# The first batch's keys turned on TensorE, and routing in two places per batch of a retention and expert kernel

## The chip, the core and the metric

The kernel runs on one core of one Trainium2 chip. The metric is the device time of one execution in microseconds (us). The program is built once and timed in several runs, of which the median is given; one more execution is recorded by the hardware profiler. The engines are TensorE (PE; its weight loads are shown apart as PEld), VectorE (DVE), ScalarE (ACT), GpSimd (POOL) and SyncE (SP), which here only issues transfers.

## The reference

Two stages follow each other. The first is a retention: causal scores with a decay per head and no softmax. The second sends each token to one of eight experts. All is float32.

```python
def _attn_ref(q, k, v):                       # q, k, v: (8, 8, 576, 64)
    scores = scale * np.matmul(q, k.transpose(0, 1, 3, 2))
    gamma = 1.0 - 2.0 ** (-5.0 - np.arange(H, dtype=np.float32))
    Dmat = np.where(rel >= 0, gamma[:, None, None] ** rel[None, :, :], 0.0)
    return np.matmul(scores * Dmat[None], v)

def _moe_ref(x, expert_emb, tau, w1, w2):     # x: (4608, 512), 8 experts, F = 1024
    logits = normalised(x) @ normalised(expert_emb).T / tau
    expert_idx = np.argmax(logits, axis=1)
    gate_w = softmax(logits)[arange, expert_idx]
    for e in range(E):
        mask = expert_idx == e
        h = np.maximum(x[mask] @ w1[e], 0.0)
        out[mask] = gate_w[mask, None] * (h @ w2[e])
```

## The kernel before

**Data.** The host lays out `qk`, in which queries and keys stand transposed (the two heads of a pair by 64 features on the 128 partitions, 576 positions along), and `kv`, in which keys and values stand by position, in chunks of 128 positions. So the keys come twice: transposed, for the scores, and by position, in the tile `kt`, for the prefix sums of k times v.

**Retention.** It runs over 8 batches `b` and in each over 4 pairs of heads `p`. `emit_A(b, p)` makes the scores within chunks of 128 positions (L563, 16 matmuls) and masks them on VectorE (L572). `emit_U(b)` multiplies keys by position with values (L590, 64 matmuls) and sums over chunks on VectorE (L602, L604) to the states `Tst`. `emit_O(b, p)` multiplies masked scores by values (L620) and states by queries (L629), and VectorE scales and stores the result (L638, or L640 and L641). `emit_At` and `emit_Ot` are the same for the last 64 positions (L650, L652; L665, L668). `scale_v(b + 1)` on GpSimd multiplies the next batch's values by decays (L547, L551), as soon as they have landed. `emit_A` for the next pair stands ahead of `emit_O` for this one, and `emit_U(b + 1)` stands at the end of batch `b`.

**Routing.** The tokens of batch `b` are routed while batch `b + 1` runs, 4 tiles of 128 tokens for even `b` and 5 for odd `b`. `route_tasks(b)` lists the tasks. `route_logits` (L707, copy L710) and `route_turn` (L720, reduction L723) give the logits by token. `route_head` is six short VectorE operations (L174 to L182) that find the expert. `route_tile` turns one tile of tokens (L687), copies it on ScalarE (L691), stores it to memory through SP (L693) and sums its squares (L695). `route_rank` counts how many tokens stand ahead of each in its expert (matmuls L233 to L237, then L240 to L260 on VectorE). `route_onehot` makes the one-hot matrices `bt`, `ra` and `rp` on VectorE (L276, L268, L283), and `route_table` multiplies them (L296) and adds the product to the slot table `tab` (L305, L307). Ranks and table go on from batch to batch, so they must be made in order of the batches.

**Where the tasks stand.** After each pair of a batch before the last, three tasks are taken from the list: logits, head and tile 0 after pair 0; rank with one-hots and two tiles after pair 1; the rest and the table after pair 2. In the last batch `POPS` = 6, 3, 4, 0 tasks are taken ahead of `emit_O`: the list of batch 6 there ends with the slots of the first three groups of expert 0, three gathers of their tokens (L335) and `route_bump`. Behind the last batch the gathered tokens are turned (`xprep`, L365) and the experts' stage begins (L392 and L836).

**What sets the order.** The kernel is written in a tile framework. It takes the instructions in program order as their priority, and puts them on each engine's queue by a model of when each is ready; so an instruction can come ahead of one that is written before it. Each engine runs its queue in order. Tiles come from pools with fixed numbers of buffers; PSUM tiles named `m` (three buffers), `a` (three) and `o` (two) matter here. The expert weights' first four pieces (`wsplit_tasks(0)`, L145, L148, L149) stand in batches 1 and 2.

Of the kernel before, what the change touches and what calls it, by code (L numbers as in the profile page):

```python
# [9 lines left out]
F32 = mybir.dt.float32  # L10
# [8 lines left out]
P = 128  # L19
B, H, S, D = 8, 8, 576, 64  # L20
NP = H // 2
NCH = 4
# [19 lines left out]
EPOS = 2  # L42
OA = None
LAG = (3, 1)
POPS = (6, 3, 4, 0)
NO = NT + 2


# [32 lines left out]
def retention_moe(ctx: ExitStack, tc: tile.TileContext, qk, kv, embT, tau, w1, w2, cst, out):  # L81
    nc = tc.nc
# [8 lines left out]
    psm = ctx.enter_context(tc.tile_pool(name="psm", bufs=3, space=PSUM))  # L91
# [31 lines left out]
    ident = keep.tile([P, P], F32, name="ident")  # L123
# [139 lines left out]
    def route_onehot(b):  # L263

        t0, G = group_tiles(b)
        ai = grp[b][0]
        bt = sm.tile([P, 5, P], BF16, name="bt", bufs=1)[:, :G]
        nc.vector.tensor_tensor(  # L268
            out=bt,
            in0=ai[:, 1].unsqueeze(2).broadcast_to([P, G, P]),  # L270
            in1=cc("iota").unsqueeze(1).broadcast_to([P, G, P]),
            op=ALU.is_equal,
        )
        ra = sm.tile([P, 5, NE, CT], F32, name="ra", bufs=1)[:, :G]
        held = cc("iota")[:, : NE * (CT + 1)].rearrange("p (e i) -> p e i", e=NE)[:, :, :CT]
        nc.vector.tensor_tensor(  # L276
            out=ra,
            in0=ai[:, 0].unsqueeze(2).unsqueeze(3).broadcast_to([P, G, NE, CT]),
            in1=held.unsqueeze(1).broadcast_to([P, G, NE, CT]),
            op=ALU.is_equal,  # L280
        )
        rp = sm.tile([P, 5, 2, NA], BF16, name="rp", bufs=1)[:, :G]
        nc.vector.tensor_tensor(  # L283
            out=rp,
            in0=ra.rearrange("p g e i -> p g (e i)").unsqueeze(2).broadcast_to([P, G, 2, NA]),
            in1=entry[:, t0 : t0 + G].unsqueeze(3).broadcast_to([P, G, 2, NA]),
            op=ALU.mult,
        )
        grp[b] = (bt, rp)
# [137 lines left out]
    with ExitStack() as att:  # L427
# [12 lines left out]
        kt, vt_ = {}, {}  # L440
        KW = NCH * DM

        def load_k(b):
            t = a1.tile([P, KW], F32, name="kt", bufs=2)
            nc.sync.dma_start(out=t, in_=kv[b, :, :KW])
            kt[b] = t
# [16 lines left out]
        load_v(0, True)  # L463
        load_qk(0, 3)
        nc.sync.dma_start(out=cs[:, _FIRST:], in_=cst[:, _FIRST:])
        load_k(0)
        nc.sync.dma_start(out=emb, in_=embT)
        nc.sync.dma_start(out=taub, in_=tau.rearrange("(o n) -> o n", o=1).broadcast_to([P, 1]))

# [63 lines left out]
        def kview(b):  # L533
            return kt[b].rearrange("p (c n) -> p c n", c=NCH)
# [7 lines left out]
        def scale_v(b):  # L542
            eng = nc.vector if b == 0 else nc.gpsimd
            g = cc("gneg").rearrange("p (c h) -> p c h", c=NCH)
            v = vview(b)
            for c in range(NCH):
                eng.tensor_tensor(  # L547
                    out=v[:, c], in0=v[:, c], in1=g[:, c].unsqueeze(2).broadcast_to([P, H, D]), op=ALU.mult
                )
            vt = vtview(b)  # L550
            eng.tensor_tensor(  # L551
                out=vt, in0=vt, in1=cc("gnegt").unsqueeze(2).broadcast_to([P, NP, D]), op=ALU.mult
            )

        Pm, Pt = {}, {}

# [142 lines left out]
        def route_logits(b):  # L699

            x = xT[b, "x"]
            lt = a1.tile([P, 5 * P], F32, name="lt")
            parts = [(x, 0, 512)] if b % 2 == 0 else [(x, P, 512), (xC[b // 2], 0, P)]
            for src, o, n in parts:
                ps = psm.tile([P, 512], F32, name="m")
                for p in range(NP):
                    nc.tensor.matmul(  # L707
                        ps[p * EW : (p + 1) * EW, :n], E32[:, p, :], src[:, p, :], start=True, stop=True
                    )
                nc.scalar.copy(lt[:, o : o + n], ps[:, :n])  # L710
            ltb[b] = lt

        def route_turn(b):
            t0, G = group_tiles(b)
            lt = ltb.pop(b)
            for g0 in range(0, G, 4):
                gn = min(4, G - g0)
                ps = psm.tile([P, 512], F32, name="m")
                for g in range(gn):
                    nc.tensor.transpose(  # L720
                        ps[:, g * P : (g + 1) * P], lt[:, (g0 + g) * P : (g0 + g + 1) * P], ident
                    )
                nc.vector.tensor_reduce(  # L723
                    out=L_all[:, t0 + g0 : t0 + g0 + gn, :],
                    in_=ps[:, : gn * P].rearrange("p (g r e) -> p g e r", g=gn, r=NP)[:, :, :NE, :],
                    axis=AX.X,
                    op=ALU.add,
                )


        def route_tasks(b):
            G = group_tiles(b)[1]
            tiles = [lambda g=g: route_tile(b, g) for g in range(G)]
            logits = lambda: (route_logits(b), route_turn(b))
            head = lambda: route_head(b)
            rank, table = (lambda: (route_rank(b), route_onehot(b))), (lambda: route_table(b))
            if b == B - 2:
                t = [logits] + tiles[:2] + [head, rank] + tiles[2:] + [table, lambda: slots_to_tokens(0, 3)]
                t += [lambda i=i: gather(0, i, group_tiles(B - 1)[0] * P) for i in range(3)]
                return t + [route_bump]  # L740
            return [logits, head, tiles[0], rank] + tiles[1:] + [table]

        tasks = []
        wq = wsplit_tasks(0)
# [5 lines left out]
        for b in range(B):  # L750
            for p in range(NP):
                if b + 1 < B:
                    load_qk(b + 1, p)
                    if p == 0:
                        load_v(b + 1)
                        load_k(b + 1)
                        scale_v(b + 1)
                if p + 1 < NP:
                    if b > 0 or p == 2:
                        emit_A(b, p + 1)  # L760
                else:
                    if b + 1 < B:
                        emit_A(b + 1, 0)
                    emit_At(b)
                    if b + 1 < B:
                        emit_U(b + 1)
                if b == 0 and p == 0:
                    emit_U(0)
                if b == 0 and p == EPOS:
                    build_E()  # L770
                for _ in range(POPS[p] if b == B - 1 else 0):
                    if tasks:
                        tasks.pop(0)()
                emit_O(b, p)
                if p == NP - 1:
                    emit_Ot(b)
                for _ in range(3 if b < B - 1 else 0):
                    if tasks:
                        tasks.pop(0)()
                if b > 0 and p % 2 == 1 and wq:  # L780
                    wq.pop(0)()
            if b < B - 1:
                tasks += route_tasks(b)
# [306 lines left out]
```

## Time and profile before

| | us |
|---|---|
| median of 3 runs | 639.4 (639.04 to 642.41) |
| profiled execution | 639.75 |
| span in its profile | 637.8 |
| TensorE matmul busy | 618.2 (97%) |
| VectorE busy | 366.7 (57%) |
| ScalarE busy | 215.5 (34%) |
| GpSimd busy | 188.8 (30%) |

The retention stage takes up the span to about 176 us; the experts' stage fills the rest. Busy time of an engine is an average over both, so a stage has to be read by its own stretch. In the rows, a bracket behind an instruction tells how long its engine had been idle before it and what ended the wait; "x16" is a merged group of 16 instructions of which the first number is the start and the second the time from the first one's start to the last one's end. The granted clock is given as a share of TensorE's full speed, 2.4 GHz; 0.5 is 1.2 GHz.

### The profile page before, as it was taken

The numbers are of one execution on the slowest core, as the hardware profiler recorded it, in microseconds if no ns is written. First come the engines' busy times: TensorE is split into PE (matmuls) and PEld (weight loads), VectorE is DVE, ScalarE is ACT, GpSimd is POOL, SyncE is SP. The second block draws the span as 40 slices with busy tenths as digits, with TensorE's granted clock in tenths as the row PEclk, the third lists the DMA queues.
The fourth block names the chain that finished last, engine by engine and source line by source line (L and its number), as shares of the span: only waits on it lengthen the run. The fifth ranks groups of instructions, "written<-read, shape, count | busy, mean of one in ns | idle before, by whom it ended". The sixth has DMA issues, their size and how long they took to land. (4 is left out here: it accounts for less than half of the span.)

```text
span 637.8 us, 12644 instructions
## 1 busy us (share of the span) xinstructions
PE 618.2 (97%) x5257; PEld 551.8 (87%) x5257; DVE 366.7 (57%) x711; ACT 215.5 (34%) x393; POOL 188.8 (30%) x167
## 2 busy tenths in 40 slices
PE   8889899999999999999999999999999999999996
PEld 7768788788889889988988998898899889889985
DVE  5799988889758676660681466158146615812200
ACT  0032433223354536432442443244244324422211
POOL 3530322032126646313503322250332225020011
PEclk9999899999999999999999999999999999999999
DMA  8778889665356697492465148246514824500001
GB/s 321 302 251 334 309 324 330 253 249 205 120 160 198 188 240 250 118 264 94 110 151 218 57 116 268 84 116 172 208 33 117 281 82 116 149 37 23 1 34 43
DMA packets 73419, 110.46 MB, mean 173 GB/s; under 512 B 44650, under 2 KB 45070, under 8 KB 71440
## 3 DMA queue, kind: packets, MB, share of 16 engines
q1 hardware_dynamic: 65680, 89.68, 43.9%
q0 software_dynamic: 7680, 19.95, 9.6%
q8 instruction: 42, 0.69, 0.4%
q14 instruction: 17, 0.14, 0.1%
HBM read 81.01 MB, written 19.94 MB: 158 GB/s over the span
## 5 line engine op out<-in xcount | busy, mean ns | idle before, releaser
L392 PE MATMUL a<-xs,wslot 128*128 128x384 f32 (+1 forms) x1536 | 228.3, 310 | 0.4 <-DVE hs L810 0.4
L392 PEld LDWEIGHTS a<-xs,wslot 128*128 128x128 f32 x1536 | 225.9, 189 | 1.5 <-DVE hs L810 0.8
L836 PE MATMUL o<-wslot,hs 128*128 128x512 f32 (+1 forms) x984 | 222.0, 386 | 0.0
L836 PEld LDWEIGHTS o<-wslot,hs 128*128 128x128 f32 x984 | 181.1, 188 | 38.3
L810 DVE SCALAR_TENSOR_TENSOR hs<-a,hs 128x384 fp32r<-128x384 f32 (+1 forms) x128 | 62.8, 491 | 169.5 <-ACT hs L809 167.0
L844 POOL DMA_INDIRECT out<-y,sid x40 | 43.4, 1084 | 221.9 <-ACT y L843 188.2
L809 ACT ACTIVATE hs<-a 128x384 fp32r<-128x384 f32 (+1 forms) x128 | 56.1, 439 | 125.8 <-PE a L392 119.7
L149 DVE TENSOR_TENSOR wslot<-raw,wslot 128x1024 fp32r<-128x1024 f32 x64 | 78.3, 1223 | 27.7 <-ACT wslot L148 27.0
L148 ACT CAST wslot<-raw 128x1024 fp32r<-128x1024 f32 x64 | 66.8, 1044 | 53.1 <-DMA raw<-w 53.1
L335 POOL DMA_INDIRECT raw<-xd,gid x40 | 44.1, 1104 | 90.8 <-DVE wslot L149 42.0
L843 ACT ACTIVATE y<-o,gt 128x512 f32<-128x512 f32 (+1 forms) x41 | 27.7, 677 | 110.2 <-PE o L836 89.1
L547 POOL TENSOR_TENSOR vt<-vt,cs 128x512 f32<-128x512 f32 x28 | 29.8, 1092 | 90.5 <-DMA vt<-kv 36.5
L346 POOL DMA_INDIRECT gt<-gd,gid x40 | 50.0, 1251 | 12.2 <-issue 12.2
L563 PE MATMUL a<-qkt 64*128 64x128 f32 x512 | 43.1, 293 | 0.5 <-DMA qkt<-qk 0.3
L572 DVE TENSOR_TENSOR raw<-a,tri 128x512 f32<-128x512 f32 x64 | 41.0, 682 | 3.3 <-PE a L563 3.1
L563 PEld LDWEIGHTS a<-qkt 64*128 64x128 f32 x512 | 35.4, 192 | 7.9 <-issue 6.3
L620 PE MATMUL o<-raw,vt 128*64 128x128 f32 x512 | 36.1, 279 | 0.7 <-DVE raw L572 0.5
L620 PEld LDWEIGHTS o<-raw,vt 128*64 128x64 f32 x512 | 27.9, 136 | 5.0 <-issue 1.2
L710 ACT COPY lt<-m 128x512 f32<-128x512 f32 (+1 forms) x12 | 5.4, 481 | 78.5 <-PE m L707 78.5
L380 DVE COPY raw<-raw 128x1024 uint16<-128x1024 uint16 x37 | 28.3, 785 | 1.8 <-DMA raw<-raw 1.7
L691 ACT COPY y<-m 128x512 f32<-128x512 f32 x34 | 19.0, 587 | 29.9 <-PE m L687 28.3
L629 PE MATMUL o<-qkt,Tst 128*64 128x128 f32 x384 | 28.4, 274 | 0.0
(131 smaller groups left out, 442.8 us busy)
## 6 DMA issues: line engine op xcount, KB each, us to landing
raw<-w SPq DMA_DIRECT2D x64, 512.0 KB
qkt<-qk SPq DMA_DIRECT2D x32, 576.0 KB
xd<-y SPq DMA_DIRECT2D x36, 256.0 KB
kt<-kv SPq DMA_DIRECT2D x8, 1024.0 KB
vt<-kv SPq DMA_DIRECT2D x7, 1152.0 KB
vt<-kv SPq DMA_DIRECT2D x4, 256.0 KB
raw<-xd,gid POOLq DMA_INDIRECT x40
gt<-gd,gid POOLq DMA_INDIRECT x40
```

The source lines that it names most:

```text
L148: nc.scalar.copy(hi, raw)
L149: nc.vector.tensor_tensor(out=sl[:, 1, c * 1024 : (c + 1) * 1024], in0=raw, in1=hi.bitcast(F32), op=ALU.subtract)
L335: return nc.gpsimd.indirect_dma_start(out=t[:, :DM], out_offset=None, in_=xd[:rows, :], in_offset=bass.IndirectOffsetOnAxis(ap=gid[:, a : ...
L346: nc.gpsimd.indirect_dma_start(out=g[:, i : i + 1], out_offset=None, in_=gd[:, :], in_offset=bass.IndirectOffsetOnAxis(ap=gid[:, a : a + 1 ...
L392: nc.tensor.matmul(ps[:, :n], w[:, ws, d, f * P : (f + 1) * P], x[:, xsp, d, :], start=(d == 0 and k == 0), stop=(d == NP - 1 and k == 2),)
L563: nc.tensor.matmul(ps[h][:, c * P : (c + 1) * P], t[hs, 1, c * P : (c + 1) * P], t[hs, 0, c * P : (c + 1) * P], start=True, stop=True,)
L572: nc.vector.tensor_tensor(out=pm[:, h], in0=ps[h].rearrange("p (c n) -> p c n", c=NCH), in1=tri.unsqueeze(1).broadcast_to([P, NCH, P]), op ...
L620: nc.tensor.matmul(po[h * D : (h + 1) * D, c * P : (c + 1) * P], v[:, c, 2 * p + h, :], pm[:, h, c, :], start=(c == 0), stop=False,)
L809: a = nc.scalar.activation(hi, ps[:, :n], AF.Relu)
L810: v = nc.vector.scalar_tensor_tensor(out=hs[:, 1, f, o : o + n], in0=ps[:, :n], scalar=0.0, in1=hi.bitcast(F32), op0=ALU.max, op1=ALU.subt ...
L836: nc.tensor.matmul(ps[:, :step], hs[:, hsp, f, i * P : (i + 1) * P], w[:, ws, f, n : n + step], start=(f == 0 and k == 0), stop=(f == NF - ...
L844: nc.gpsimd.indirect_dma_start(out=out[:, :], out_offset=bass.IndirectOffsetOnAxis(ap=sid[:, a : a + 1], axis=0), in_=y, in_offset=None, b ...
```

## The change

`kt[0]`, the first batch's keys by position, is no longer loaded. The tile stays, and `turn_k` fills it: for each pair, four transposes on TensorE of the keys in `qkt[0, p]` into one PSUM tile and one copy on ScalarE. It stands at batch 0, pair 0, ahead of `emit_U(0)`.

The routing tasks of a batch now stand at two pairs of the next one, `SLOTS` = 0 and 2. At pair 0: rank and one-hots of the batch *before* the one that is being routed, then logits and tiles 0 and 1. At pair 2: the table of the batch before, then turn, head and the rest of the tiles. So rank, one-hots and table come a batch later than head and tiles. The list of batch 6, which runs in the last batch, takes batch 5's rank and table in as well, and `POPS` is 8 in place of 6.

```diff
-POPS = (6, 3, 4, 0)
+POPS = (8, 3, 4, 0)
+SLOTS = (0, 2)
...
-        load_k(0)
+        kt[0] = a1.tile([P, KW], F32, name="kt", bufs=2)
...
+        def turn_k(p):
+
+            ps = psm.tile([P, 512], F32, name="m")
+            for c in range(NCH):
+                nc.tensor.transpose(ps[:, c * P : (c + 1) * P], qkt[0, p][:, 1, c * P : (c + 1) * P], ident)
+            nc.scalar.copy(kview(0)[:, :, p * P : (p + 1) * P], ps.rearrange("p (c n) -> p c n", c=NCH))
...
+        owed = []
+
         def route_tasks(b):
             G = group_tiles(b)[1]
             tiles = [lambda g=g: route_tile(b, g) for g in range(G)]
-            logits = lambda: (route_logits(b), route_turn(b))
             head = lambda: route_head(b)
             rank, table = (lambda: (route_rank(b), route_onehot(b))), (lambda: route_table(b))
+            own = [lambda: route_logits(b)] + tiles[:2], [lambda: route_turn(b), head] + tiles[2:]
+
+            first, second = owed or ([], [])
+            owed[:] = [rank], [table]
             if b == B - 2:
-                t = [logits] + tiles[:2] + [head, rank] + tiles[2:] + [table, lambda: slots_to_tokens(0, 3)]
+                t = first + [lambda: (route_logits(b), route_turn(b))] + second + tiles[:2] + [head, rank]
+                t += tiles[2:] + [table, lambda: slots_to_tokens(0, 3)]
                 t += [lambda i=i: gather(0, i, group_tiles(B - 1)[0] * P) for i in range(3)]
                 return t + [route_bump]
-            return [logits, head, tiles[0], rank] + tiles[1:] + [table]
+            return [first + own[0], second + own[1]]
...
                 if b == 0 and p == 0:
+                    for r in range(NP):
+                        turn_k(r)
                     emit_U(0)
...
-                for _ in range(3 if b < B - 1 else 0):
-                    if tasks:
-                        tasks.pop(0)()
+                if b < B - 1 and p in SLOTS and tasks:
+                    for task in tasks.pop(0):
+                        task()
```

## Rows read from the trace of the kernel before

**Rows 1.** Page, part 1: busy us, share of the span, instructions, by engine.
```profile
PE 618.2 (97%) x5257; PEld 551.8 (87%) x5257; DVE 366.7 (57%) x711; ACT 215.5 (34%) x393; POOL 188.8 (30%) x167
```

**Rows 2.** Busy time by stretches, one per batch; last three: clock, DMA share, GB/s.
```profile
33.08:54.11 21.03, 19.74 (x324) 16.51 (x324) 19.95 (x46) 6.67 (x14) 5.15 (x5) 1.00 0.85 303
54.11:77.91 23.80, 22.07 (x342) 18.82 (x340) 22.57 (x49) 8.90 (x19) 5.36 (x5) 0.93 0.88 312
77.91:96.80 18.89, 18.80 (x327) 16.05 (x325) 16.47 (x45) 6.67 (x14) 4.68 (x5) 1.00 0.84 304
96.80:118.63 21.83, 20.32 (x342) 17.37 (x341) 18.89 (x43) 7.00 (x17) 5.67 (x5) 1.00 0.75 273
...
137.52:159.12 21.60, 20.32 (x343) 17.37 (x341) 18.66 (x43) 6.91 (x17) 4.75 (x5) 1.00 0.62 227
```

**Rows 3.** Groups by line, TensorE: busy us, mean ns, idle us before, releaser.
```profile
L296 PE MATMUL m<-rp,bt 128*128 128x80 bf16 x36 | 2.6, 203 | 5.6 <-DVE rp L283 5.6
```

**Rows 4.** Timeline, five tiles routed: start us, us, engine, line, operation.
```profile
107.53 4.77 POOL L547 TENSOR_TENSOR vt<-vt,cs 128x512 f32<-128x512 f32 x4 [13.11 <-PE m L687]
...
111.32 1.41 DVE L283 TENSOR_TENSOR rp<-ra,entry 128x400 bf16<-128x400 f32 x1
...
112.79 0.35 PE L296 MATMUL m<-rp,bt 128*128 128x80 bf16 x5 [1.49 <-DVE rp L283]
...
113.07 1.47 PE L563 MATMUL a<-qkt 64*128 64x128 f32 x16
```

**Rows 5.** Timeline, four tiles routed.
```profile
89.74 4.11 POOL L547 TENSOR_TENSOR vt<-vt,cs 128x512 f32<-128x512 f32 x4 [19.78 <-DMA vt<-kv]
...
90.82 0.42 PEld L687 LDWEIGHTS m<-ident,xT 128*128 128x128 f32 x4 [0.17 <-issue]
...
91.32 0.31 PE L296 MATMUL m<-rp,bt 128*128 128x80 bf16 x4
...
91.55 1.16 PE L563 MATMUL a<-qkt 64*128 64x128 f32 x16
```

**Rows 6.** Busy time behind one of the stops, columns as in rows 2.
```profile
70.45:74.90 4.45, 4.29 (x55) 3.79 (x57) 4.18 (x7) 3.36 (x7) 0.00 (x0) 0.62 0.90 351
```

**Rows 7.** Single lines to 175 us: duration ns as minimum/median/maximum.
```profile
L259 DVE TENSOR_SCALAR ai<-si x7: 170/898/975, 43.9 to 166.3; 128x4 int32<-128x4 int32 x4, 128x5 int32<-128x5 int32 x3
...
L276 DVE TENSOR_TENSOR ra<-ai,cs x7: 324/1123/1165, 44.8 to 166.5; 128x160 f32<-128x160 int32 x4, 128x200 f32<-128x200 int32 x3
...
L268 DVE TENSOR_TENSOR bt<-ai,cs x7: 683/1230/1660, 45.9 to 166.7; 128x512 bf16<-128x512 int32 x4, 128x640 bf16<-128x640 int32 x3
...
L283 DVE TENSOR_TENSOR rp<-ra,entry x7: 482/896/1408, 47.3 to 167.3; 128x320 bf16<-128x320 f32 x4, 128x400 bf16<-128x400 f32 x3
...
L531 DVE TENSOR_TENSOR E<-emb,en x4: 649/900/1076, 27.6 to 30.2; 128x8 f32<-128x8 f32 x4
...
L175 DVE TENSOR_TENSOR L_all<-L_all,mx x7: 191/194/201, 41.2 to 164.3; 128x32 f32<-128x32 f32 x4, 128x40 f32<-128x40 f32 x3
```

**Rows 8.** Timeline of batch 0.
```profile
17.70 2.09 PE L590 MATMUL m<-vt,kt 128*64 128x64 f32 x64 [1.50 <-DMA kt<-kv]
...
27.60 3.30 DVE L531 TENSOR_TENSOR E<-emb,en 128x8 f32<-128x8 f32 x4
...
33.08 0.33 PE L665 MATMUL m<-pt,vt 64*64 64x64 f32 x4 [1.82 <-DVE pt L652]
```

**Rows 9.** Waits of SP's queue to 150 us: total, times, longest.
```profile
SPq L693 <- ACT y L691: 58.8, 18, 6.8
```

**Rows 10.** Busy time of two stretches, columns as in rows 2.
```profile
8.00:15.04 7.04, 5.88 (x65) 4.66 (x65) 5.55 (x10) 0.00 (x0) 0.75 (x1) 1.00 1.05 404
...
159.12:172.42 13.30, 13.26 (x194) 10.81 (x194) 11.51 (x39) 5.53 (x13) 0.00 (x0) 1.00 0.35 124
```

**Rows 11.** Timeline at the end of the retention stage.
```profile
172.42 1.19 POOL L335 DMA_INDIRECT raw<-xd,gid  x1 [20.37 <-DVE raw L572]
...
177.55 1.09 PE L365 MATMUL m<-ident,raw 128*128 128x128 f32 x8
```

## Prediction

> **What bounds the kernel now.** I read the page's first part first: TensorE is busy for 97% of the span and every other engine for far less [rows 1]. So the time is a row of TensorE work, and a change pays only where TensorE stands still or runs at its lower clock, or where it takes work off that engine. This change takes none off it (it adds 16 transposes), so I looked for the stops. The busy time by stretches, one stretch per batch of the retention stage (each from the first matmul of the last-rows product of one batch to that of the next), is the second view [rows 2]. The reader is to see two kinds of batch. A batch in which four token tiles are routed takes 18.89 us with TensorE busy for all but 0.09. A batch in which five are routed takes 21.60 or 21.83 with 1.3 to 1.5 us idle, the one from 54.11 takes 23.80, and batch 1, with four tiles, takes 21.03. The excess is what the change can reach; there are three batches with five tiles and batch 1.
>
> The third view, the groups by line, says what TensorE stood still for: before L296, the slot table's matmuls, it was idle for 5.6 us in all, released by `rp` of L283 on VectorE [rows 3]. The timeline shows that this is four stops, of which one stands in the rows [rows 4]. There GpSimd runs `scale_v` from 107.53 on, VectorE's one-hot steps run beside it, `rp` ends at 112.73, and only then can L296 start, 1.49 us late. In a four-tile batch [rows 5] the same L296 starts at 91.32 with no wait. The difference lies in VectorE's steps: L259, L276, L268 and L283 take 0.17, 0.32, 0.68 and 0.48 us at best, but 0.98, 1.17, 1.66 and 1.41 at worst [rows 7], and the worst stand beside `scale_v`. The work in the odd batches is one tile more, which does not make 0.32 into 1.17.
>
> The Trainium skill, "SBUF — State Buffer", section "Who interferes with whom", gives the reason: VectorE and GpSimd share one port pair as an exclusive lock, and a VectorE operation with two inputs in SBUF, or in a two-port mode, waits out the whole GpSimd instruction. The trace agrees where `scale_v` runs (0.32 against 1.17).
>
> **The change part by part.** *The four stops.* Rank and one-hots go to the first slot (p = 0) of the batch after, the table's matmuls to its third (p = 2), some 9 us later. `rp` is then long there. GpSimd's window lies at 9.6 to 12 us after a batch's start and runs to 16 (89.74 less 77.91 is 11.8, the four operations of 4.11 us end at 15.9) [rows 2, 5], and the one-hots now run at about 3 to 8 us, in front of it. So the wait goes: 5.6 us. Its lower bound is 0, if the order on the engines puts the steps back side by side.
>
> *What follows a stop.* The mask product A behind it takes 1.47 us instead of 1.16 [rows 4, 5], as the masks queue behind `rp` on VectorE and hold its PSUM buffers. Three times 0.31 is 0.9 us. The fourth falls into the next term.
>
> *The lower clock.* After the stop in the batch from 54.11 the granted clock averages 0.62 for 4.45 us [rows 6], that is mostly the 1.2 GHz level. At 2.4 GHz these 4.45 us would shorten by at most 4.45 x 0.38 = 1.7. Before it fell, TensorE had stood still for 1.5 us; the other stops were followed by no fall. Without the stop I count the 1.7 as gained, with 0 as the other end, as a fall can come elsewhere.
>
> *The first batch's keys.* Removed is one load of 1 MB, for which TensorE waited 1.50 us before the first product of L590 [rows 8]. Added are 16 transposes. Four of them take 0.42 us on TensorE [rows 5], so 1.7 in all, and four ScalarE copies, on an engine that does nothing then. From 8.00 to 15.04 TensorE is idle for 1.16 us [rows 10], in pieces, and the first three key tiles are there by then, as A has read them. So about 0.5 us is not covered, and 1.50 less 0.5 leaves 1.0 us. If all is covered it is 1.5; if nothing is, and the fourth tile's copy is waited for, it is -0.8. Behind it VectorE's prefix sums, and so the state products, come earlier by the same amount. All loads behind it land earlier by the load's share, which no wait of TensorE asks for before 30 us.
>
> *The p = 2 slot.* Logits are turned and the head is made there now, beside two or three tiles. TensorE's amount is the same. The products of p = 2 ended at 90.82, that is 12.9 us after the batch's start [rows 2, 5], so the head would come at about 14, in the last 2 us of GpSimd's window. Today the head never meets it (L175: 0.19 us median, 0.20 at most [rows 7]), so its cost there is not shown. The nearest row is L531, four small operations with two SBUF inputs beside `scale_v`: 0.90 us median [rows 7], 0.7 more than the 0.19 that L175 takes free. Two of the four at 0.7 are 1.4 us of VectorE, and it has 18.89 - 16.47 = 2.4 us idle in such a batch [rows 2], while the rank steps beside it get shorter. I take 1.0 us for all six batches, for PSUM buffers freed late. The ends are 0 and 10.9 (below). Nothing gains by it.
>
> *SP's and GpSimd's queues.* The token stores go out two at p = 0 and two or three at p = 2, instead of one, two and the rest. SP waited 58.8 us on ScalarE's copies before them [rows 9], with the loads of the next queries behind; these are used a batch later, so I put the cost at 0. If that cover went, a query load late by one wait is a stop of the same size. `scale_v` stays where it was.
>
> *The end of the stage.* Batch 7 gets the rank, one-hots and table of batch 5 on top of those of batch 6, with POPS 8 in place of 6. The four large steps free are 1.65 us and six short ones at 0.2 make 1.2, so 2.85 us of VectorE. It is idle for 1.79 us from 159.12 to the first gather at 172.42 [rows 10]. So the first gather may come 1.06 us later. TensorE takes the gathered rows at 177.55 without a wait [rows 11]. I take 0.8 us lost; ends 0 and 2.9.
>
> **The sum.** 5.6 + 0.9 + 1.7 + 1.0 - 1.0 - 0.8 = 7.4 us. The profiled execution took 639.75 (span 637.8 and 1.95 around it), so 632.35; the median of the runs is 0.35 lower, which gives 632.0. The experts' stage behind carries the gain, as TensorE is gap-free there and nothing in it is timed from the start of the program.
>
> **The rivals.**
> (1) *The head in GpSimd's window*, the side on which it is slower. Batch 0 shows this case: the four operations of L531 beside `scale_v` last from 27.60 to 30.90, the last-rows mask comes late behind them, and TensorE waits 1.82 us at 33.08 [rows 8]. If the head met the window whole, each of six batches would lose that: 10.9 in place of the 1.0. Then 632.0 + 9.9 = 641.9, and with a clock that falls again (1.7) 643.6. It decides from the point where the head starts before about 12 us into a batch. For it: two inputs in SBUF. Against: 14 us by the rows, and 2.4 us of idle VectorE.
> By the Trainium skill, "SBUF — State Buffer", section "Who interferes with whom", this would hold for L175, L177, L181 and L182 but not for the reductions L174 and L179, which never contend; no run here shows the head beside `scale_v`.
> (2) *The seam gives it back*: batch 7's gathers come late by the whole 2.9 us and TensorE, standing still, loses its clock as it did after 68.95 (1.7). 632.0 + 2.1 + 1.7 = 635.8. For it: tables are added in order, so batch 5's stands in front of batch 6's. Against: VectorE's idle 1.79.
> (3) *It doesn't do what it says*: the order on each engine is not the program's (A of the fourth pair ran before the first prefix product of L590), and rank and table could be set next to each other again, or the turned keys be put in front of products that are ready. Two of four stops stay (2.8 + 0.5), the clock falls (1.7), and batch 0 gives -0.8 for 1.0: 632.0 + 6.8 = 638.8.
>
> **How the numbers follow.** Forecast 0.66, between 628.5 and 635; (1) 0.12; (2) 0.12; (3) 0.10. A measurement of this kernel can tell about 0.5% from no change, 3.2 us, so faster means below 636.2 and slower above 642.6. Faster: 0.66 + 0.09 of (2) + 0.03 of (3) = 0.78. Slower: 0.07 of (1) and 0.01 of (3), 0.08. Same: 0.14. The range runs from 628, where all terms are at their good ends (5.6 + 0.9 + 1.7 + 1.5 = 9.7 gives 629.7, less 1.7 for terms I have not seen), to 638, which takes in (2) and part of (3) and leaves out (1).
>
> **What would show it.** Right: no idle time before L296; batches of 19 and 20 us by turns, batch 1 below 19.5; the clock at 1.0 from 70 to 75; L590 starting near 16.7; one-hot steps at their short times. Wrong: idle time before L650, L590 or L665 in each batch with the head's operations at 0.9 us (1), idle time before L365 or a fall of the clock at 175 to 182 (2), L296 still behind L283 (3).

## The result, and the profile of the changed kernel

The changed kernel takes 632.76 us (median of 4 runs, 632.15 to 634.07), the kernel before, measured beside it, 639.76 (639.04 to 642.41). The ratio is 0.9887, with a 95% interval of 0.9852 to 0.9921: 7 us faster, against 632.0 forecast, in a range of 628 to 638. The profiled execution took 633.18, with a span of 631.2 (before: 639.75 and 637.8).

The total is near the forecast. Its terms are not, and most of what follows is about that.

The stretches first, cut as in [rows 2], from the last-rows product of one batch (here L673) to that of the next; the first begins with the first product of scores. Columns: stretch and length, then busy us (instructions) of PE, PEld, DVE, ACT, POOL, then clock, DMA share, GB/s.

```profile
5.42:30.93 25.51, 24.42 (x377) 21.57 (x376) 17.48 (x43) 2.15 (x4) 10.77 (x10) 1.00 0.84 306
30.93:49.37 18.44, 17.97 (x315) 15.42 (x313) 15.43 (x34) 6.31 (x14) 4.62 (x5) 1.00 0.97 363
49.37:71.28 21.91, 19.69 (x338) 16.80 (x338) 19.47 (x48) 8.68 (x19) 4.62 (x5) 1.00 0.83 301
71.28:91.75 20.47, 19.30 (x330) 16.27 (x328) 18.23 (x42) 6.60 (x14) 4.62 (x5) 1.00 0.83 300
91.75:112.02 20.27, 19.64 (x341) 16.82 (x339) 18.18 (x47) 6.68 (x17) 4.62 (x5) 1.00 0.81 292
...
131.10:150.79 19.69, 19.69 (x341) 16.80 (x339) 16.81 (x45) 6.76 (x17) 4.62 (x5) 1.00 0.69 249
150.79:169.03 18.24, 18.04 (x259) 14.49 (x258) 15.30 (x54) 5.40 (x13) 2.85 (x3) 1.00 0.32 109
```

The stretches of the kernel before that [rows 2] leaves out, of batches 0 and 7 (batch 5 is like batch 3 before, and its row is left out here too):

```profile
5.43:33.08 27.65, 22.82 (x357) 19.31 (x357) 20.67 (x40) 0.00 (x0) 10.74 (x10) 1.00 0.81 315
...
159.12:175.86 16.74, 16.33 (x248) 13.43 (x247) 13.22 (x44) 5.53 (x13) 2.83 (x3) 1.00 0.35 118
```

Length less the first busy time is TensorE's idle time. Set beside [rows 2]:

| batch | length before | after | difference | TensorE idle before | after |
|---|---|---|---|---|---|
| 0 | 27.65 | 25.51 | -2.14 | 4.83 | 1.09 |
| 1 | 21.03 | 18.44 | -2.59 | 1.29 | 0.47 |
| 2 | 23.80 | 21.91 | -1.89 | 1.73 | 2.22 |
| 3 | 18.89 | 20.47 | +1.58 | 0.09 | 1.17 |
| 4 | 21.83 | 20.27 | -1.56 | 1.51 | 0.63 |
| 5 | 18.89 | 19.08 | +0.19 | 0.09 | 0.00 |
| 6 | 21.60 | 19.69 | -1.91 | 1.28 | 0.00 |
| 7 | 16.74 | 18.24 | +1.50 | 0.41 | 0.20 |
| sum | 170.43 | 163.61 | -6.82 | 11.23 | 5.78 |

5.45 us come from idle time, 1.37 from busy time, although the 16 added transposes are in it; batch 2 alone is busy 2.38 us less, since its clock was 0.93 before and is 1.00 now. The lead of 6.82 us is carried to the end almost whole: the spans differ by 6.6, and the token turns that open the next stage start at 170.77 instead of 177.55 [rows 11].

The reader is to see that idle time has not simply gone. In batches 2 and 3 there is more of it than before. The groups by line (columns: busy us, mean ns, then idle us before them) have the table's line, L297, which is L296 before:

```profile
L297 PE MATMUL m<-rp,bt 128*128 128x80 bf16 x31 | 2.3, 205 | 0.0
```

Its 5.6 us of idle time [rows 3] are 0.0. But L695, which turns token tiles, now waits for VectorE's L248, a step of the rank, where no such wait stood before. The waits by releaser count three (columns: total us, times, longest); they stand in batches 2, 3 and 4 and take 1.74, 1.17 and 0.63 us:

```profile
PE m L695 <- DVE t L248: 3.5, 3, 1.7
```

### The profile page after: what moved, and what is told of

Its sections match the earlier page's. It is cut to its first block, busy times and chain, and to the rows that moved or that the text cites. A ratio compares the mean times of both kernels' runs of the same rounds, so it can differ in the third digit from the quotient of the medians.

```text
span 631.2 us, 12686 instructions
## 1 busy us (share of the span) xinstructions
PE 616.8 (98%) x5273; PEld 551.4 (87%) x5273; DVE 357.1 (57%) x711; ACT 216.2 (34%) x397; POOL 183.5 (29%) x167
## 5 line engine op out<-in xcount | busy, mean ns | idle before, releaser
L336 POOL DMA_INDIRECT raw<-xd,gid x40 | 41.9, 1047 | 90.3 <-DVE wslot L150 42.9
L548 POOL TENSOR_TENSOR vt<-vt,cs 128x512 f32<-128x512 f32 x28 | 28.4, 1044 | 90.2 <-DMA vt<-kv 64.1
L381 DVE COPY raw<-raw 128x1024 uint16<-128x1024 uint16 x37 | 28.2, 786 | 3.9 <-DMA raw<-raw 3.4
L374 DVE COPY raw<-raw 128x1024 uint16<-128x1024 uint16 x37 | 26.0, 718 | 0.0
```

Source lines behind the costliest of these rows:

```text
L336: return nc.gpsimd.indirect_dma_start(out=t[:, :DM], out_offset=None, in_=xd[:rows, :], in_offset=bass.IndirectOffsetOnAxis(ap=gid[:, a : ...
```

## The experiments

The runs come in three groups of four kernels, each group on one chip, and each kernel is set against runs of the kernel before on its own chip. "After" is the changed kernel. The medians of the kernel before were 639.88 us beside the first four, 642.11 beside the next four, 641.43 beside the last four. A profile shows one execution, whose time is given below where it lies far from the median.

| run | kernel | median us | ratio to before, 95% interval |
|---|---|---|---|
| e0_before_again | before, profiled execution alone | 639.95 | |
| e1_keys | before, keys turned | 636.11 | 0.9945 (0.9921 to 0.9968) |
| e2_routing | after, keys loaded | 635.83 | 0.9914 (0.9884 to 0.9944) |
| e8_table_later | before, only L296 a batch later | 646.30 | 1.0109 (1.0071 to 1.0147) |
| e3_rank_behind | after, ranks behind tiles | 631.19 | 0.9853 (0.9819 to 0.9887) |
| e6_rank_only | the same, turn held behind O | 631.33 | 0.9860 (0.9821 to 0.9898) |
| e7_head_only | after, turn and head a pair earlier | 636.33 | 0.9922 (0.9890 to 0.9953) |
| e9_emb_later | before, embedding after pair 3 | 640.17 | 0.9964 (0.9929 to 1.0000) |
| e10_after_again | after | 635.18 | 0.9914 (0.9887 to 0.9940) |
| e11_rank_emb | e3, embedding after pair 3 | 632.43 | 0.9861 (0.9833 to 0.9889) |
| e12_loaded_emb | e11, keys loaded | 631.25 | 0.9852 (0.9825 to 0.9878) |
| e5_both | e3 and e7 together | 639.65 | 0.9986 (0.9951 to 1.0022) |

### e0: the kernel before once more

> The kernel before, unchanged, recorded a second time. Theory A (the fall of TensorE's clock in the batch from 54.11 belongs to the kernel): granted clock about 0.93 in the same stretch and 23.8 us for that batch. Theory B (a fall comes by chance after such a stop): the fall stands elsewhere or nowhere, that batch is about 21.8 us, and the span is some 1.7 us shorter. The four stops before L296 (5.6 us) stand in both.

It took 639.95 us. The stretches of batches 1 and 2:

```profile
32.74:54.85 22.11, 21.06 (x325) 17.88 (x325) 20.21 (x47) 6.67 (x14) 4.62 (x5) 0.92 0.79 288
54.85:78.38 23.53, 21.77 (x342) 18.70 (x340) 22.21 (x48) 8.88 (x19) 5.32 (x5) 0.93 0.89 317
```

In [rows 2] the clock of batch 1 was 1.00 and that of batch 2 was 0.93. So the fall in batch 2 came again, behind the stop before L296 there (1.74 us at 71.08), as theory A says, and another came in addition, at 34 us, behind the 1.82 us stop before L665, which [rows 8] has too, without a fall behind it. The 1.7 us booked for batch 2 stand in both executions; how many falls an execution has is not fixed.

### e1: the keys alone

```diff
-        load_k(0)
+        kt[0] = a1.tile([P, KW], F32, name="kt", bufs=2)
...
+                    for r in range(NP):
+                        turn_k(r)
                     emit_U(0)
```

> Keys of the first batch turned on TensorE, routing as before. Theory A (the first batch's gain is its own and does not hang on the routing): batch 0 about 2.2 us shorter as in the changed kernel, with the first matmul of L590's product later than 17.70, not earlier, and no wait for the last-rows mask at its end; time about 637.5. Theory B (the first batch is shorter because of the new routing's order): no change, 639.7.

636.11 us, so 3.8 less than before, though the routing stands as it was and I had given this part 1.0. Batch 0 takes 25.54 us, 2.1 less. The profiled execution is the fastest of ten (633.61 us). In it the rest is in the stops, of which only two are left:

```profile
PE m L296 <- DVE rp L283: 2.5, 2, 1.3
```

The reason stands in the timeline of VectorE and GpSimd (two views; start us, us):

```profile
103.02 0.37 DVE L276 TENSOR_TENSOR ra<-ai,cs 128x200 f32<-128x200 int32 x1
103.30 1.67 DVE L268 TENSOR_TENSOR bt<-ai,cs 128x640 bf16<-128x640 int32 x1
104.89 1.41 DVE L283 TENSOR_TENSOR rp<-ra,entry 128x400 bf16<-128x400 f32 x1
...
103.04 4.16 POOL L547 TENSOR_TENSOR vt<-vt,cs 128x512 f32<-128x512 f32 x3 [13.68 <-DMA vt<-kv]
```

`scale_v` starts at 103.04, when its values have landed. The step ahead of that instant is short (0.37), those behind it are long (1.67, 1.41). One load less in batch 0 has moved the two against each other by a fraction of a microsecond, and that is enough for a stop to vanish. In this execution the two halves of the change thus reach partly for the same stops.

### e2: the routing alone

```diff
-        kt[0] = a1.tile([P, KW], F32, name="kt", bufs=2)
+        load_k(0)
...
-                    for r in range(NP):
-                        turn_k(r)
                     emit_U(0)
```

> Routing in two places with ranks and table a batch later, first keys loaded as before. Theory A: the gain of 4.5 us from batches 1 to 7 stands alone, batch 0 takes its 27.65 us; time about 635.2. Theory B (the two parts share a gain): more or less than that by over 1.5 us.

635.83 us. The stops before the table are gone, the waits behind L248 are there, and in batch 0 the wait for the last-rows mask, which the changed kernel no longer has, is back:

```profile
PE m L695 <- DVE t L248: 2.2, 3, 1.4
...
PE m L673 <- DVE pt L660: 1.8, 1, 1.8
```

The two gains by ratio, 0.55% and 0.86%, add up to 1.41%, where the whole has 1.13%; with intervals of about 0.3% each, that is no difference that can be told. A cost of one part that hides in the gain of the other is not seen.

### e8: only the stop is taken away

Here L296 alone goes a batch later. Ranks and one-hots stay where they were, beside `scale_v`, and TensorE no longer waits for `rp`.

```diff
+            prior = owed[0] if owed else (lambda: None)
...
-            logits = lambda: (route_logits(b), route_turn(b))
+            logits = lambda: (prior(), route_logits(b), route_turn(b))
...
+            owed[:] = [table]
-            return [logits, head, tiles[0], rank] + tiles[1:] + [table]
+            return [logits, head, tiles[0], rank] + tiles[1:]
```

> Only the table's matmuls (L296) stand a batch later; ranks, one-hots and head stay where they were, beside scale_v on GpSimd. Theory A (the stop itself was the price, 5.6 us and 0.9 behind it, and 1.7 of clock): about 631.5. Theory B (VectorE beside scale_v was the price and the stop only showed it): VectorE's one-hots stay at 1.2 to 1.7 us, the masks queue behind them, TensorE stops a step later, and about half of it stays: 635.5 or more.

646.30 us, 6.4 slower than before. The wait has only changed its name:

```profile
PE a L563 <- DVE raw L572: 5.0, 6, 1.7
```

One of the six in the timeline:

```profile
45.34 3.13 POOL L547 TENSOR_TENSOR vt<-vt,cs 128x512 f32<-128x512 f32 x3
45.44 0.97 DVE L259 TENSOR_SCALAR ai<-si 128x4 int32<-128x4 int32 x1
...
46.45 1.12 DVE L276 TENSOR_TENSOR ra<-ai,cs 128x160 f32<-128x160 int32 x1
...
47.49 1.53 DVE L268 TENSOR_TENSOR bt<-ai,cs 128x512 bf16<-128x512 int32 x1
...
48.94 0.90 DVE L283 TENSOR_TENSOR rp<-ra,entry 128x320 bf16<-128x320 f32 x1
49.76 1.27 DVE L572 TENSOR_TENSOR raw<-a,tri 128x512 f32<-128x512 f32 x2
50.49 1.84 PE L563 MATMUL a<-qkt 64*128 64x128 f32 x14 [1.73 <-DVE raw L572]
```

The mask L572 stands behind the long one-hots on VectorE, and holds the PSUM buffer of the scores. So taking the stop away does not help: VectorE falls behind beside `scale_v`, and L296 was only the first to notice. In e2 and after, where the one-hots stand elsewhere and are short, neither line waits for them. The counterpart, one-hots moved and the table's matmuls kept right behind them, was not run.

The waits explain that nothing was gained, not the whole loss. The profiled execution is the fastest of the four, 641.59 us, and TensorE's idle time in it is not longer than in the kernel before; its clock is lower, 0.94, 0.86 and 0.93 in batches 0, 1 and 6, where before it is below 1.00 in batch 2 alone. The other three runs took 645.71 to 648.51 us, and what they lost there is not recorded.

### e3 and e6: the ranks behind logits and tiles

In the first slot of the changed kernel the rank's product takes a buffer of the pool `m`, ahead of the logits and two token tiles, which take the next ones. The pool has three. If that is the cause of the waits at L695, letting the ranks go last must end them.

```diff
-            return [first + own[0], second + own[1]]
+            return [own[0] + first, second + own[1]]
```

> The changed kernel with rank and one-hots listed behind logits and the two tiles of the first slot, not in front. The order that results also puts the turn of the logits, and so the head, at pair 1 and not at pair 2. Both theories: the 3.5 us that TensorE waits for rank's PSUM buffer (tile turns behind L248) go, and the head's operations are at 0.2 us; 629.5, against 633 for the changed kernel.

e6 has the same edit, and besides holds turn and head back explicitly, behind the last product of pair 2's `emit_O`:

```diff
+        def turn_late(b):
+            with after(lastO[b + 1, 2]):
+                route_turn(b)
...
-            own = [lambda: route_logits(b)] + tiles[:2], [lambda: route_turn(b), head] + tiles[2:]
+            own = [lambda: route_logits(b)] + tiles[:2], [lambda: turn_late(b), head] + tiles[2:]
```

> The changed kernel with rank behind the two tiles, and the turn of the logits held behind the products of pair 2, so that the head stays beside scale_v. Theory A (the 3.5 us are a matter of PSUM buffers: rank's tile is one of three and is read late): they go, 629.8. Theory B (VectorE is late because the head stands beside scale_v, and the wait would go elsewhere): 632.5 or more, with waits before L650, L665 or L707 in their place.

631.19 and 631.33 us, ratios 0.9853 and 0.9860. The expectation of e3 says that turn and head would move to pair 1 by themselves; in the trace they did not (L728 starts at 103.10, after the table's L297), so the two kernels are one experiment done twice. The longest line of e6's waits:

```profile
PE a L571 <- DVE raw L580: 1.3, 2, 0.9
```

No wait behind L248 is left in either. The head still meets `scale_v` in e6:

```profile
102.61 4.04 POOL L548 TENSOR_TENSOR vt<-vt,cs 128x512 f32<-128x512 f32 x4 [14.21 <-DMA vt<-kv]
...
104.71 1.00 DVE L176 TENSOR_TENSOR L_all<-L_all,mx 128x40 f32<-128x40 f32 x1
105.74 0.97 DVE L178 SCALAR_TENSOR_TENSOR w<-L_all,wme 128x40 f32<-128x40 f32 x1
```

so the order of the PSUM buffers is the cause of the new waits, and the head beside `scale_v` is not.

What these waits cost in time is less clear. By ratio e3 and e6 lie 0.3% below after, which is within the intervals. In the profiled executions batches 1 to 6 take 119.66 us in e3 and 120.26 in e6, against 119.86 in after: what is gained before L695 is lost elsewhere in the same batches. Part of it is not idle time at all. In e3 the masks on VectorE follow the one-hots directly, and a group of scores is stretched (e3, then after, both in batch 5):

```profile
119.44 1.61 PE L571 MATMUL a<-qkt 64*128 64x128 f32 x16
```

```profile
120.90 1.16 PE L571 MATMUL a<-qkt 64*128 64x128 f32 x16
```

What e3 and e6 have less lies in batch 0 (24.75 and 24.40 us against 25.51) and in batch 7 (17.71 in both against 18.24), where the edit moves nothing; after itself took 17.70 in batch 7 when it was profiled again (e10).

### e7: the head a pair earlier

```diff
-SLOTS = (0, 2)
+SLOTS = (0, 1, 2)
...
-            own = [lambda: route_logits(b)] + tiles[:2], [lambda: route_turn(b), head] + tiles[2:]
+            own = [lambda: logits_behind(b)] + tiles[:2], [lambda: route_turn(b), head], tiles[2:]
```

`logits_behind` keeps the logits behind the rank's last product, so that the ranks stay first as in the changed kernel.

> The changed kernel with turn and head at pair 1, in front of scale_v, and rank held in front of the logits as in the changed kernel. Theory A (PSUM buffers): the waits behind L248 stay for the most part (2.5 us or more of 3.5), about 632. Theory B (head beside scale_v makes VectorE late): the waits go with the late head, 629.8.

636.33 us, ratio 0.9922. The waits grew (all lines are two further down here):

```profile
PE m L697 <- DVE tab L310: 3.4, 2, 2.1
PE m L697 <- DVE t L250: 3.1, 2, 1.7
PE m L697 <- DVE tab L308: 2.2, 1, 2.2
```

With turn and head gone from the third slot, the token tiles there come right behind the table's product, and now wait for its buffer too, which the table's addition on VectorE (`tab`) frees. It is the same mistake a second time, in the other slot. The waits behind the rank (L250 here) stay at 3.1 us although the head is gone from pair 2, which bears out e3 and e6; the time that theory A gave, 632 us, is missed because of the table.

### e9: batch 0 without turned keys

The prediction had batch 0 gain from the keys. In the trace of after, the sums of L598 start no earlier (19.18, against 17.70 in [rows 8]) and still batch 0 is 2.14 us shorter. The other candidate is the order on VectorE. GpSimd's short step for the expert embedding, L528, and `scale_v(1)` have changed places (before, then after):

```profile
24.61 1.67 POOL L527 TENSOR_TENSOR en<-en,half 128x8 f32<-128x8 f32 x1 [5.84 <-DVE en L526]
26.27 4.04 POOL L547 TENSOR_TENSOR vt<-vt,cs 128x512 f32<-128x512 f32 x4
```

```profile
19.50 4.05 POOL L548 TENSOR_TENSOR vt<-vt,cs 128x512 f32<-128x512 f32 x4 [0.74 <-DMA vt<-kv]
...
26.50 0.41 DVE L660 TENSOR_TENSOR pt<-m,trit 128x256 f32<-128x256 f32 x1
26.67 1.67 POOL L528 TENSOR_TENSOR en<-en,half 128x8 f32<-128x8 f32 x1 [2.55 <-DVE en L527]
...
28.87 0.40 DVE L532 TENSOR_TENSOR E<-emb,en 128x8 f32<-128x8 f32 x4
```

The four steps of L532 take 0.40 us together instead of 3.30 [rows 8], and the mask L660 stands ahead of them. e9 brings about that order in the kernel before, with its loaded keys:

```diff
-EPOS = 2
+EPOS = 3
```

> The kernel before with EPOS 3 in place of 2: the expert embeddings are normalised after the last-rows mask of batch 0 and not ahead of it; the first keys are still loaded. Theory A (batch 0 gains because the mask no longer queues behind L531's four operations beside scale_v): the 1.82 us wait at the end of batch 0 goes, 637.9. Theory B (it gains because the load of 1 MB is gone): no change, 639.7.

Its batch 0 takes 25.52 us, 2.1 less than before, although the clock was 0.93 there, and the last-rows products wait for nothing at its end; the wait for the loaded keys was 0.6 us this time. Over the whole kernel the ratio is 0.9964, about 2 us, with an interval that just reaches no change. The stops before L296 remain, 5.5 us in five places. So the order of batch 0 is worth about 2 us, with or without turned keys.

### e10, e11, e12: turned or loaded keys once the order is right, and after again

e11 is e3 with `EPOS = 3`; e12 is e11 with `load_k(0)` in place of `turn_k`.

> The changed kernel, unchanged, as the measure for the other three on the same chip. Its span by batches and its stops should come again: 3 to 4 us before the tile turns L695 behind the rank's PSUM buffer (L248), no stop before L297, batch 0 near 25.5 us. Time near 632.8 us (631.5 to 634.5). If the stops behind L248 were a chance of one execution, as the clock's falls were in the kernel before, they would stand at other places or be below 1 us in all.

> The changed kernel with the ranks behind logits and tiles in their slot (as in the run that gave 631.2 us), and with the products of the experts' embedding made after pair 3 instead of pair 2 of batch 0. Theory 'order of batch 0 is settled': with turned keys the last-rows mask already stands ahead of the embedding's steps, so the later place gives nothing: 631.2 us, between 630.4 and 632, batch 0 24.4 to 24.9 us. Rival 'the steps still lie in the way beside scale_v(1)': batch 0 loses another 0.5 us or more, 630.6 us or less. On the losing side: the steps now run in batch 1, beside its states, and batch 1 grows above 19.2 us: 632 us.

> The same as the kernel with the ranks behind and the embedding after pair 3, but with the first batch's keys loaded from memory as before, not turned on TensorE. Theory 'the turned keys have a worth of their own': the first product of L591 waits for the load for about 1.5 us, against 1.7 us of transposes that it no longer makes but that lay in gaps; the clock may fall behind it; batch 0 1 to 1.5 us longer than with turned keys, about 632.5 us. Rival 'only the order of batch 0 counted': the load's wait and the transposes cost the same, both kernels within 0.5 us of each other, about 631.2 us. If loading is better, 630.5 us or less.

After took 635.18 us on this chip (634.05 to 635.73), e11 632.43 (631.09 to 633.72), e12 631.25 (630.67 to 631.70). e11 and e12 lie apart from after, on one chip; they differ from it in the place of the embedding too, so this bears out e3 without repeating it. In the second profile of after the stops behind L248 are two, 1.74 and 0.57 us, fewer than the expected 3 to 4 us, and none stands before L297. Between them loading is not worse, and in the profiled executions better by 2.9 us of span (628.7 against 631.6). Batch 0 holds 1.9 us of that (26.95 us in e11, where 24.4 to 24.9 were expected, and 25.09 in e12). The stretch from 12 to 14 us shows where; after, e11, e12 on this chip in turn:

```profile
12.00:14.00 2.00, 2.00 (x13) 1.67 (x13) 2.00 (x5) 1.41 (x3) 0.00 (x0) 0.50 0.99 266
```

```profile
12.00:14.00 2.00, 2.00 (x11) 1.78 (x10) 2.00 (x5) 0.57 (x1) 0.00 (x0) 0.52 1.09 330
```

```profile
12.00:14.00 2.00, 1.50 (x23) 1.10 (x19) 2.00 (x5) 0.00 (x0) 0.77 (x1) 1.00 1.09 446
```

The clock fell to its lower level during the turning of the keys. In the profile of after on the first chip it stood at 1.00 in the same stretch, and in e2, with loaded keys, it was at 0.50 from 12 to 16 us. Over all profiled executions it fell in batch 0 in 3 of 8 with turned keys and in 3 of 6 with loaded ones, so the turned keys are not shown to be the reason. They are not cleared either: all three with turned keys on this chip fell and e12 did not, while on the other chips none of five fell. The fastest runs of e11 and e12, with mean granted clocks of 0.998 and 0.999, took 631.09 and 630.67 us, 0.4 apart. The load's wait is still there in e12, and yet its sums start earlier than any with turned keys:

```profile
16.56 2.09 PE L591 MATMUL m<-vt,kt 128*64 128x64 f32 x64 [1.30 <-DMA kt<-kv]
```

1.30 us waited for stand against 16 transposes of 2.4 us busy. So these runs show no worth of the turned keys of their own; what they did was to bring the values of batch 1 in sooner, so that `scale_v(1)` got ahead of L528, and moving the embedding does that as well. The expectation of a loss of 1 to 1.5 us for e12 was wrong.

### e5: ranks behind, and the head a pair earlier

```diff
-SLOTS = (0, 2)
+SLOTS = (0, 1, 2)
...
-            own = [lambda: route_logits(b)] + tiles[:2], [lambda: route_turn(b), head] + tiles[2:]
+            own = [lambda: route_logits(b)] + tiles[:2], [lambda: route_turn(b), head], tiles[2:]
...
-            return [first + own[0], second + own[1]]
+            return [own[0] + first, own[1], second + own[2]]
```

> The changed kernel with three slots: after pair 0 logits, two tiles and then the ranks; after pair 1 turn and head; after pair 2 the table of the batch before and the other tiles. So the head is moved ahead of GpSimd's scale_v, and the ranks stay behind the tiles. Theory 'VectorE's lag behind the head is hidden by TensorE's queue': nothing to gain over the kernel with only the ranks moved, 631.2 us (630.4 to 632.2). Rival 'the head beside scale_v delays the masks': 1 us or more less, 630 us or lower, with the operations of L176, L178 and L182 below 0.35 us in all batches. On the losing side: the tile turns after pair 2 wait for the table's PSUM buffer, as in the run with the head alone moved, and it takes 633 us or more.

639.65 us, hardly faster than before. The losing side of the expectation came true, with 8.8 us of waits and the clock at 0.87 and 0.86 in batches 2 and 4 of the profiled execution, which took 644.69 us.

```profile
PE m L695 <- DVE tab L308: 5.5, 2, 2.8
PE m L695 <- DVE tab L306: 3.3, 1, 3.3
```

The timeline of one shows how an addition of 0.22 us is waited for that long:

```profile
106.24 4.04 POOL L548 TENSOR_TENSOR vt<-vt,cs 128x512 f32<-128x512 f32 x4 [14.04 <-DMA vt<-kv]
106.26 1.09 DVE L178 SCALAR_TENSOR_TENSOR w<-L_all,wme 128x40 f32<-128x40 f32 x1
...
107.61 0.32 PE L297 MATMUL m<-rp,bt 128*128 128x80 bf16 x4
...
111.16 0.22 DVE L308 TENSOR_TENSOR tab<-m,tab 128x80 f32<-128x80 f32 x1
...
111.44 1.12 PE L695 MATMUL m<-ident,xT 128*128 128x128 f32 x4 [2.61 <-DVE tab L308]
```

L297 is done at 107.93; L308 runs 3.2 us later, at the end of a VectorE queue with head, masks and scaling in it. And the head is long here even at pair 1 (L178 1.09 us), because `scale_v` starts when its load lands, not at a fixed place.

## Why the prediction came out, step by step

**Where TensorE stands still: right.** The view by batches and the groups by line pointed to the idle time, and 5.45 of 6.82 us came from there.

**The four stops, 5.6 us: right.** L297 waits for 0.0. The one-hots take their short times in every batch (L277 0.32 to 0.37 us, L284 0.48 to 0.57). e8 sharpens the reason: the kernel that takes away the wait without moving the one-hots is 6.4 us slower. The prediction named the one-hot steps beside `scale_v` as what made `rp` late; it did not say that this, not the wait, had to be got rid of.

**A behind a stop, 0.9, and the clock, 1.7: right in this execution, the clock not in general.** The busy time of batches 1 to 7 fell by 2.97 us, 2.38 of it in batch 2, against 2.6 forecast. The fall in batch 2 belongs to both profiles of the kernel before. But e0 has another one in batch 1, and e10 has two in the changed kernel, one of them in batch 2 as well, behind a stop at L695. A sum should not have booked one fall as a fixed term.

**The first batch's keys, 1.0: size near, reason wrong.** "The fourth tile's copy is waited for" was my bad end, and it is nearly what happened: the fourth pair's transposes run at 18.60, behind two groups of scores (15.57, 17.51), so L598 starts at 19.18 and not at 16.7. Batch 0 gained 2.14 us all the same, through the order of GpSimd and VectorE, which is the 1.82 us wait of [rows 8] gone. I had that row, and had used it only as the price for rival (1). e9 and e12 settle this. The transposes were also priced too low: the 0.42 us for four of them [rows 5] is a row of weight loads (PEld). On TensorE itself four take 0.66 us in after, and all 16 are busy for 2.4 us, not 1.7.

**The p = 2 slot, -1.0: mis-sized and at the wrong place.** TensorE waited 3.5 us for PSUM buffers, in the other slot, p = 0. I had asked what the head does to VectorE, not what the rank's product does to the three buffers of `m` when two token tiles follow it. e3 and e6 take these waits away. Their medians are 1.5 us below after's, but on different chips, and their profiles do not show the gain in the batches where the waits stood; e11, which also has the embedding later, gains 2.75 against after on one chip. The head's own share of the term is small (rival (1) below).

**The end of the stage, -0.8: nothing lost.** Batch 7 is 1.50 us longer because the rank and table of batch 5 now stand in it (TensorE busy 18.04 instead of 16.33); most of that is moved work, and batch 1, which now has neither rank nor table, is busy 1.77 us less. The tokens' turn starts 1.74 us after the first last-rows product of batch 7, against 1.69 before. In e10, the same kernel, TensorE waits 0.7 us for the gathered rows (L366), so the term is not always nothing.

**The sum.** Batch 0 gave 2.1 us, the four stops 5.6, the busy time of the other batches 3.0: 10.7. The waits behind L248 took 3.5, other idle time 0.4: 6.8, as the stretches show. Forecast were 5.6 + 0.9 + 1.7 + 1.0 = 9.2 of gains and 1.8 of losses. Both sides were too small, by 1.5 and 2.1 us, and the errors cancel: the total came out closer than its terms.

**Rival (1), the head in GpSimd's window:** the condition came true in five of six batches; the price shows in one of them, well below 1.82 us. The head runs beside `scale_v` (41.69 to 45.74) in batch 1 of after:

```profile
43.23 0.19 DVE L175 TENSOR_REDUCE mx<-L_all 128x4 f32<-128x32 f32 x1
43.45 0.34 DVE L176 TENSOR_TENSOR L_all<-L_all,mx 128x32 f32<-128x32 f32 x1
43.82 0.97 DVE L178 SCALAR_TENSOR_TENSOR w<-L_all,wme 128x32 f32<-128x32 f32 x1
...
45.04 0.75 DVE L182 TENSOR_TENSOR oh<-wm,wme 128x32 bf16<-128x32 f32 x1
```

Against their short times of about 0.2 us L176, L178 and L182 lose 1.4 to 1.5 us together, the amount forecast for VectorE; in batches 3 to 6 they lose 0.6 to 1.8 us, and in batch 2 nothing. TensorE's only idle time in batch 1 is the wait that the rival names, for the last-rows mask at its end:

```profile
49.37 0.33 PE L673 MATMUL m<-pt,vt 64*64 64x64 f32 x4 [0.47 <-DVE pt L660]
```

It comes again in e10, e3 and e6 (0.82, 0.75 and 0.54 us), and it is gone in e5 and e7, where the head of batch 1 ran before `scale_v` in its short times. So the head costs about 0.5 us there, where the rival gave 1.82. In batch 5 it loses 1.75 us and TensorE stands still for none of it; that TensorE had work queued which needs nothing of the head is my reading. The Trainium skill, "SBUF — State Buffer", section "Who interferes with whom", has reductions exempt from this; the trace agrees: the reduction L175 takes 0.19 us inside the window.

**Rivals (2) and (3)** did not come: the seam kept the gain, and the table's matmuls wait for nothing in their new place. A part of (2) can be seen in other executions: TensorE waits for the gathered rows 0.7 us in e10, 1.5 and 1.7 us in e11 and e12. Of the other signs, batch 1 came below 19.5 us and the clock stayed at 1.00 from 70 to 75 us, but the batches were not 19 and 20 us by turns, and L590 did not start near 16.7.

## What to carry to other kernels

When a wait is to be removed, ask what made the producer late and move that: moving only the consumer lets the next instruction behind the same engine wait instead (e8, 6.4 us slower). When a product is moved ahead of others that share its PSUM pool, find the instruction that frees its buffer and what stands before that one on its engine; with a product that is read late in front, the work behind it stops (3.5 us of waits behind the ranks in after, gone in e3 and e6; 8.8 us behind the table in e5). But count the time and not the waits alone: in e3 and e6 the batches with the waits became hardly shorter. Loads, short GpSimd steps and embedding work of the first batch decide an order on the engines, and an edit that seems to act by its own cost may act by that order: try the order by itself before keeping the edit.

## What the runs showed of the hardware

The price of VectorE work beside GpSimd. In e8 L259, L276, L268 and L283 took 0.97, 1.12, 1.53 and 0.90 us beside `scale_v`, where the same four steps of the changed kernel take 0.17, 0.33, 0.68 and 0.48. In e1 the price sets in with the very instruction that follows the start of `scale_v` (0.37, then 1.67).

The clock. One program, the changed kernel, ran its batches 0 and 2 at 1.00 in one profiled execution and at 0.93 in the other (e10), on another chip. In batch 2 the fall followed a stop of 1.74 us, which the first execution had too, without a fall. In batch 0 none of the stops between 8 us and the fall was longer than 0.37 us. e10's four runs, with a mean granted clock of 0.990 to 0.993, took 634.05 to 635.73 us; those of the first measurement, at 0.997 and 0.998, 632.15 to 634.07. What decides in which execution the clock falls stays open.

The two lowest medians are those of e3 (631.19 us) and e12 (631.25); e12 lies clearly below after on its chip, e3 lies below it by ratio within the intervals. A pool of its own for the rank's and the table's products wasn't tried.
